# Second layer of the expert by seven products of halves, its weights' sums formed in the third chunk

## The chip, the cores and the metric

The kernel runs on one core of a Trainium2 chip. A core has a tensor engine for matmuls (PE, its weight loads shown apart as PEld), a vector engine (DVE), a scalar engine (ACT), GpSimd (POOL) and SyncE (SP), which issues nearly all DMAs here. The engines share a memory on the chip (SBUF) and the accumulators of the matmuls (PSUM, used here as banks of 128 x 512 floats). Each engine works through its own instructions in the order in which they were written, and waits on semaphores for the others. The metric is the device time of one execution in microseconds (us).

## What is computed

First an attention with a window of 32 positions and 32 global tokens (8 batches, 8 heads, head size 64). Then, on its 4608 output rows of 512 numbers, an RMS norm and a gated layer in float32:

```python
rms = np.sqrt(np.mean(x * x, axis=-1, keepdims=True) + 1e-06)
xn = x / rms * rms_g
g = xn @ w_gate                      # 512 x 1536
silu = g * (1.0 / (1.0 + np.exp(-g)))
val = xn @ w_val                     # 512 x 1536
return (silu * val @ w_out).astype(np.float32)   # w_out: 1536 x 512
```

"First layer" means the products with `w_gate` and `w_val` below, "second layer" that with `w_out`.

## The kernel before

**Numbers in halves of precision.** Every operand of a large product is held as two fp16 parts, a high one and a low one (what the high one leaves out). A product is three matmuls: high by high, low by high, high by low.

**Chunks.** The rows go in nine chunks, counted from 0: chunks 0 to 7 have 512 local rows each, chunk 8 the 256 global rows. So the fourth chunk is chunk 3, and `EARLY` (2) is the third. Chunk 0 and the attention of chunks 0 and 1 stand in an order written out by hand (`ORDER`). From chunk 1 on a loop at L1455 writes a list of work items for PE per chunk: first-layer items and then second-layer items. Between two items, `slot` (L1406) issues the steps of the next chunks' attention that are due; then come the steps of the next chunk's norm (`at`), what takes the item's result out of PSUM (`rest`), and the delayed steps of the pair before (`tail`).

**First layer of chunks 2 to 7** (`moe_pair`, L1088). A pair g of two 128-wide blocks f of the 1536 columns is done by seven products of halves, in the order 6, 1, 5, 7, 2, 3, 4, one work item each of 12 matmuls with 256 columns (L1108). The products share three banks: 7 and 4 go on top of 6, 3 on top of 5, 2 on top of 1, after ACT or DVE has read the value under them (L1124 to L1154). Their weights' sums were formed in chunk 1 and stored in HBM (`fold`, `wd`); `fetch` (L1079) brings them back, four tiles a pair, into the twelve buffers `wf`, which also hold the intermediate results s, u and v. `feed` (L1450) issues the fetches at fixed items.

**Between the layers.** A pair's tail runs at the items of the next pair: `gate` (L1158, DVE), `inner` (L1162, DVE, times the constant c_h and v), `high` (L1170, ACT) and `low` (L158, POOL through the helper `sub`; L156 where it is DVE). The last pair's tail runs in the first items of the second layer.

**Second layer** (`moe_block`, L1258). For each of the four blocks of 128 rows six items of two f, six matmuls of 512 columns each (L1266), with the weights `wo` that stay in SBUF; 24 items a chunk. `store` scales the result (L1277 on ACT, L1279 on DVE) and sends 256 KB to HBM.

**Attention of later chunks.** A local unit (`local_halves`) has loads, scores S (L665), four softmax quarters (M and N on DVE, L613; E and F on ACT, L627; D on DVE and POOL, L642; T, a transpose on DVE, L647), values A and B (L708) and the copies X and Y (L720, L721). `UNIT` says from which item on a unit may start, counted from the start of the chunk before its own, so that a negative number lies at the end of the chunk two before. S comes 8 items after the loads, the quarters 3 items apart, A 2 items after the last T. Each chunk has two such units and one of the global rows (`global_unit`).

**The norm of the next chunk** stands in the second layer at fixed distances from the chunk's end (`NORMS`): sums (L942, L944 on DVE), a matmul L953 with the root on DVE behind it (L954 to L958), then scaling, sums of halves and their two parts (`norm_halves`).

## Time and profile before

| | us |
|---|---|
| median of three runs | 934.9 |
| the three runs | 934.9, 935.76, 933.84 |
| span of the profiled execution, first to last instruction | 930.2 |
| chunk 4, first layer (488.1 to 553.4) | 65.3 |
| chunk 4, second layer (553.4 to 588.3) | 34.9 |
| chunk 7, second layer (847.9 to 879.1) | 31.2 |

The profile shows one execution. Its page gives the span from the first to the last instruction, not that execution's own time; the three times are 3.6 to 5.6 us above the span. A row of a group reads: line, engine, operation, output<-inputs, shapes, count | busy us, mean ns of one | idle time of the engine before them, and whom it waited for. In a row by line, three numbers with strokes are the shortest, the median and the longest duration in ns. In a timeline a row begins with the start and the length in us. In a row of stretches stand the stretch, its length, the busy time of each engine with the number of instructions, the granted clock of PE, the DMA share and GB/s. Consecutive instructions of DVE overlap a little: one starts before the other's recorded end.

### The profile page before, as it was taken

The page shows a single profiled execution, that of the slowest core. Times are in us where ns is not written, and L with a number is a line of the kernel's source. Part 1 is how long each engine was busy: PE and PEld are TensorE (multiplying, and loading weights), DVE is VectorE, ACT ScalarE, POOL GpSimd, SP SyncE. Part 2 cuts the span into 40 slices and gives each one's busy share as a digit, 9 for nine tenths or more (in the row PEclk, how much of TensorE's full clock was granted, in tenths as well). Part 3 has the DMA queues.
Part 4 walks back from the last instruction along what each step waited for, and adds up shares of the span by engine and source line. Part 5 has one row for each costly group of instructions (what it writes and reads, how often), then busy time and mean ns, then how long its engine had stood idle before and what let it go on. Part 6 is the DMA issues. An engine that isn't in the chain of part 4 may idle for free.

```text
span 930.2 us, 26398 instructions
## 1 busy us (share of the span) xinstructions
PE 893.9 (96%) x11028; PEld 612.2 (66%) x11028; DVE 634.0 (68%) x1603; ACT 495.4 (53%) x1232; POOL 253.8 (27%) x219
## 2 busy tenths in 40 slices
PE   5489999999999999999999999999999999999998
PEld 4444455545447885688648874788568865886584
DVE  6999987887884588557775679357846774664331
ACT  6999994555443564456344655356445732543131
POOL 0000000142423262334332353236233432332020
PEclk9699999999999999999999999999999999999999
DMA  9972533686449854495609771685349632787000
GB/s 352 407 288 96 159 120 115 209 265 198 144 119 320 282 180 147 133 299 169 213 24 279 242 238 43 200 279 184 139 136 297 190 95 79 248 273 238 35 1 23
DMA packets 83495, 173.40 MB, mean 186 GB/s; under 512 B 6705, under 2 KB 25393, under 8 KB 83377
## 3 DMA queue, kind: packets, MB, share of 16 engines
q1 hardware_dynamic: 82944, 171.40, 56.1%
q8 instruction: 86, 1.41, 0.6%
q10 hardware_dynamic: 432, 0.33, 0.1%
q14 instruction: 33, 0.26, 0.1%
HBM read 150.21 MB, written 21.50 MB: 185 GB/s over the span
## 4 chain that ended last, share of the span: by engine, by line
PE 82%; DVE 8%; DMA 4%; ACT 3%; issue 1%; POOL 1%; ACTq 0%; DVEq 0%; POOLq 0%
PE pq L1108 36%; PE po L1266 23%; PE p L1205 9%; PE a L708 4%; PE po L1333 3%; PE s L665 3%; DMA k<-in_qk_dram 2%; DMA v<-in_vw_dram 1%; DMA wr<-in_w_in_dram 1%; PE ga L838 1%; PE gs L781 1%; PE gt L824 1%; DVE wf L373 1%; ACT wr L272 1%; DVE t L1302 1%
## 5 line engine op out<-in xcount | busy, mean ns | idle before, releaser
L1108 PEld LDWEIGHTS <-wt 128*128 128x128 f16 x3024 | 292.6, 98 | 40.9 <-issue 5.3
L1266 PE MATMUL po<-wo,h 128*128 128x512 f16 x1080 | 236.2, 379 | 0.0
L1108 PE MATMUL pq<-xh,wt 128*128 128x256 f16 x1152 | 204.3, 273 | 0.0
L1266 PEld LDWEIGHTS <-h 128*128 128x128 f16 x1080 | 105.2, 98 | 123.9 <-issue 1.0
L1108 PE MATMUL pq<-xl,wt 128*128 128x256 f16 x576 | 157.0, 273 | 0.0
L1108 PE MATMUL pq<-ht,wt 128*128 128x256 f16 x1296 | 155.6, 273 | 0.9 <-issue 0.9
L642 POOL TENSOR_TENSOR e<-e,sm 128x512 f32<-128x512 f32 x48 | 50.0, 1042 | 291.4 <-DVE sm L641 287.6
L158 POOL TENSOR_TENSOR h<-t,h 128x512 f16<-128x512 f32 (+1 forms) x90 | 102.4, 1145 | 95.1 <-ACT h L1248 54.2
L1205 PE MATMUL p<-xh,wf 128*128 128x512 f16 x384 | 119.4, 382 | 6.9 <-DVE t L1302 6.3
L1205 PEld LDWEIGHTS <-wf 128*128 128x128 f16 x576 | 55.9, 99 | 74.4 <-issue 12.4
L1140 POOL TENSOR_TENSOR s<-s,s 128x512 f32<-128x512 f32 x36 | 48.2, 1339 | 190.6 <-ACT s L1137 117.9
L627 ACT ACTIVATE e<-e,sm 128x128 f32<-128x128 f32 x192 | 75.2, 393 | 36.6 <-DVE sm L613 36.5
L1170 ACT CAST h<-t 128x512 f16<-128x512 f32 x72 | 44.4, 616 | 57.3 <-DVE t L1162 56.7
L1205 PE MATMUL p<-xl,wf 128*128 128x512 f16 x192 | 73.5, 383 | 0.0
L1162 DVE SCALAR_TENSOR_TENSOR t<-t,c_h,v 128x512 f32<-128x512 f32 x72 | 70.7, 989 | 0.0
L1151 ACT ACTIVATE t<-u,half_inv 128x512 f32<-128x512 f32 x72 | 48.1, 715 | 38.7 <-DVE u L1126 28.6
L1126 DVE TENSOR_TENSOR v<-pq,s 128x512 f32<-128x512 f32 x72 | 49.6, 689 | 24.5 <-PE pq L1108 23.8
L1139 DVE TENSOR_TENSOR s<-pq,s 128x512 f32<-128x512 f32 x36 | 24.9, 691 | 44.3 <-PE pq L1108 42.2
L1133 ACT COPY s<-pq 128x512 f32<-128x512 f32 x36 | 21.0, 584 | 51.3 <-PE pq L1108 51.3
L613 DVE CUSTOM_DVE_ANT_0 e<-s,maskb 128x128 f32<-128x128 f32 x192 | 45.8, 278 | 2.8 <-PE s L665 2.8
L1126 DVE TENSOR_TENSOR u<-pq,s 128x512 f32<-128x512 f32 x36 | 24.9, 691 | 32.9 <-PE pq L1108 24.5
L1158 DVE SCALAR_TENSOR_TENSOR t<-t,u 128x512 f32<-128x512 f32 x72 | 46.9, 679 | 0.5 <-ACT t L1151 0.5
(352 smaller groups left out, 1281.5 us busy)
## 6 DMA issues: line engine op xcount, KB each, us to landing
wt<-wd SPq DMA_DIRECT2D x120, 512.0 KB, 4.8
wr<-in_w_in_dram SPq DMA_DIRECT2D x24, 512.0 KB, 9.9
k<-in_qkb_dram SPq DMA_DIRECT2D x24, 448.0 KB, 6.6
gkq<-in_gkq_dram SPq DMA_DIRECT2D x16, 576.0 KB, 6.5
wt<-wd SPq DMA_DIRECT2D x36, 256.0 KB, 4.7
out_dram<-o SPq DMA_DIRECT2D x34, 256.0 KB, 2.1
v<-in_vb_dram SPq DMA_DIRECT2D x24, 352.0 KB, 7.1
v<-in_vw_dram SPq DMA_DIRECT2D x16, 512.0 KB, 9.7
```

Source lines behind the costliest of these rows:

```text
L158: nc.gpsimd.tensor_tensor(dst, a, b, ALU.subtract)
L613: nc.vector.tensor_tensor_reduce(out=e[:, g, :], in0=ps[:, g * P : (g + 1) * P], in1=late["mask"][:, m * P : (m + 1) * P], scale=-0.125, s ...
L627: nc.scalar.activation(e[:, g, :], e[:, g, :], AF.Exp, bias=sm[:, 0, j + g : j + g + 1], scale=-1.0, accum_out=sm[:, 1, j + g : j + g + 1],)
L642: nc.gpsimd.tensor_tensor(e, e, r.unsqueeze(2).to_broadcast([P, 4, P]), ALU.mult)
L1108: nc.tensor.matmul(ps[:, j * HT : (j + 1) * HT], w[:, j, i, k * P : (k + 1) * P], x[:, k * HT : (k + 1) * HT], start=first, stop=(p in end ...
L1126: nc.vector.tensor_tensor(o, ps, x.rearrange("p (j n) -> p j n", j=2), ALU.add)
L1140: nc.gpsimd.tensor_tensor(s(6), s(6), s(1), ALU.add)
L1151: nc.scalar.activation(t, st["u"][:, j, :], AF.Tanh, scale=half_inv[:, f : f + 1])
L1158: nc.vector.scalar_tensor_tensor(t, t, 1.0, u, ALU.add, ALU.mult)
L1162: nc.vector.scalar_tensor_tensor(t, t, c_h[:, f : f + 1], st["v"][:, j, :], ALU.mult, ALU.mult)
L1205: nc.tensor.matmul(ps[:, :n], rows[:, a, o : o + P], ch[z][k][:, :n], start=(k == 0 and i == 0), stop=(k == NK - 1 and i == 2),)
L1266: nc.tensor.matmul(ps[0], ch["h", f][:, a, j * P : (j + 1) * P], wo[f][:, z, :], start=(f == 0 and q == 0), stop=(f == NF - 1 and q == 2),)
```

## The change

From chunk 3 on, the second layer is done by seven products of halves too (`moe_out`): a block (p, g) of the list `BLOCKS` is six matmuls with 256 columns (three in chunk 8), and a work item has two blocks, so 21 items a chunk instead of 24. Products 1, 5 and 6 run side by side over g; then 2 goes on top of 1's bank, 7 on 6, 3 on 5, 4 on 6. ACT takes out 1, 6 and 2, DVE adds the others (`rest`). The stationary operand is a half of the inner values or one of four sums of halves (`out_parts`): DVE forms the sums, ACT takes the high parts, POOL the low ones (DVE for the last pair). The moving operand is a tile of the weights: a half of `wo` or a sum of halves. These sums are formed in chunk 2 (`fold_out`: POOL, DVE, ACT, POOL) and stored in HBM with the plain halves (`wa`, `wb`); `fetch_out` brings them back in eleven fetches a chunk. All fetches now have a due item, nine items ahead (`LEAD`), 19 in chunk 8. The results are stored in two transfers of 512 KB. Two powers of two in the scaling are changed, and attention's starts move from -26, 2, 12 to -29, -1, 9.

```diff
-    UNIT = {2: (0, 20), 3: (-26, 2, 12)}
+    UNIT = {2: (0, 20), 3: (-29, -1, 9)}
     FOLD = 6
+    LEAD = 9
...
-        nc.vector.tensor_scalar(x2, g2[:, 1:2], ginv, 2.0**-16, ALU.mult, ALU.mult)
+        nc.vector.tensor_scalar(x2, g2[:, 1:2], ginv, 2.0**-14, ALU.mult, ALU.mult)
...
-        power(gp[0], 1, 15, k_o)
+        power(gp[0], 1, 13, k_o)
...
+    wa = dram.tile([P, NF // 2, 3, 2, HT], F16, tag="wa", bufs=1, name="wa")
+    wb = dram.tile([P, 4, NF // 2, 2, HT], F16, tag="wb", bufs=1, name="wb")
+    ALONG, AFTER = (1, 5, 6), (2, 7, 3, 4)
+    BLOCKS = [(p, g) for g in range(NF // 2) for p in ALONG]
+    BLOCKS += [(p, g) for p in AFTER for g in range(NF // 2)]
+
+    def fold_out(g):
+
+        st = {}
+
+        def total():
+            w = wo[2 * g][:, 0], wo[2 * g + 1][:, 0]
+            t = st["t"] = pool.tile([P, 1024], F32, tag="wo", bufs=7, name=f"os{g}")
+            for j in range(2):
+                nc.gpsimd.tensor_tensor(
+                    t[:, j * DM : (j + 1) * DM], wo[2 * g + j][:, 0], wo[2 * g + j][:, 1], ALU.add
+                )
+
+        def sums():
+            a = st["t"].rearrange("p (q n) -> p q n", q=4)
+            for q, r in ((0, 1), (1, 3), (3, 0), (2, 3)):
+                x, y = (a[:, r], a[:, q]) if q < 2 else (a[:, q], a[:, r])
+                nc.vector.tensor_tensor(a[:, q], x, y, ALU.subtract)
+
+        def high():
+            d = pool.tile([P, 4, 2, HT], F16, tag="wf", bufs=NF, name=f"od{g}")
+            st["d"] = d
+            nc.scalar.copy(d[:, :, 0, :], st["t"].rearrange("p (q n) -> p q n", q=4))
+
+        def low():
+            d = st["d"]
+            sub("P", d[:, :, 1, :], st["t"].rearrange("p (q n) -> p q n", q=4), d[:, :, 0, :])
+
+        def store():
+            d = st["d"]
+            nc.sync.dma_start(wa[:, g, 1:3], d[:, 0::3])
+            nc.sync.dma_start(wb[:, 1::2, g], d[:, 1:3])
+            nc.sync.dma_start(wa[:, g, 0], wo[2 * g][:, :, :HT])
+            for z in range(2):
+                w = wo[2 * g + 1][:, :, z * HT : (z + 1) * HT]
+                nc.sync.dma_start(wb[:, 2 * z, g], w)
+
+        return {0: total, 2: sums, 4: high, 5: low, 8: store}
...
-    def moe_pair(ch, g):
+    def fetch_out(c, k):
+        t = pool.tile([P, 4, 2, HT], F16, tag="wf", bufs=NF, name=f"wu{c}_{k}")
+        if k < 5:
+            n = min(4, 18 - 4 * k)
+            src = wa.rearrange("p g q a n -> p (g q) a n")[:, 4 * k : 4 * k + n]
+        else:
+            n = 4
+            src = wb.rearrange("p q g a n -> p (q g) a n")[:, 4 * k - 20 : 4 * k - 16]
+        nc.sync.dma_start(t[:, :n], src)
+        for i in range(n):
+            chunks[c]["wu", (4 * k if k < 5 else 4 * k - 2) + i] = t[:, i]
+
+    def moe_pair(ch, g, parts):
...
+        def formed(j):
+            f, v = 2 * g + j, st["v"][:, j, :]
+            nc.vector.scalar_tensor_tensor(
+                v, st["t", j], c_h[:, f : f + 1], v, ALU.mult, ALU.mult
+            )
+
+        sums, units, splits = out_parts(ch, g, lambda: (st["v"], st["u"]), SL)
...
-        if g == NF // 2 - 1:
+        if parts:
+            ch["tail", g] = [
+                lambda: (gate(0), gate(1)),
+                lambda: (formed(0), formed(1)),
+                lambda: (sums(0), units(0)),
+                lambda: (sums(1), units("P")),
+                lambda: splits(0),
+                lambda: splits("P"),
+            ]
+            if g == NF // 2 - 1:
+                ch["tail", g] = [
+                    lambda: (gate(0), gate(1)),
+                    lambda: (formed(0), formed(1)),
+                    lambda: (sums(0), sums(1), units(0)),
+                    lambda: (splits(0), units("P")),
+                    lambda: splits("V"),
+                    lambda: None,
+                ]
+        elif g == NF // 2 - 1:
...
+    def out_parts(ch, g, tiles, n):
+
+        w, st = n // 2, {}
+
+        def of(t):
+            return t.rearrange("p j (z n) -> p j z n", z=2)
+
+        def sums(i):
+            v, s = (of(t) for t in tiles())
+            if i == 0:
+                nc.vector.tensor_tensor(s[:, 0, 0], v[:, 0, 1], v[:, 1, 1], ALU.add)
+                nc.vector.tensor_tensor(s[:, 1, 0], v[:, 0, 0], v[:, 0, 1], ALU.subtract)
+            else:
+                nc.vector.tensor_tensor(s[:, 0, 1], s[:, 0, 0], v[:, 0, 0], ALU.subtract)
+                nc.vector.tensor_tensor(s[:, 1, 1], v[:, 1, 0], s[:, 0, 1], ALU.subtract)
...
+        def units(on):
+            v = tiles()[0]
+            if not on:
+                hi, lo = st["u"] = both("hu", "wo", 7)
+                for j in range(2):
+                    ch.setdefault("hp", {})[1 + j, g] = [x[:, j, :w] for x in (hi, lo)]
+                ch["hp"][4, g] = [x[:, 1, w:] for x in (hi, lo)]
+                nc.scalar.copy(hi, v)
+            else:
+                hi, lo = st["u"]
+                sub(on, lo[:, :, :w], v[:, :, :w], hi[:, :, :w])
+                sub(on, lo[:, 1, w:], v[:, 1, w:], hi[:, 1, w:])
+
+        def splits(on):
+            s = tiles()[1]
+            if not on:
+                hi, lo = st["s"] = both("hs", "h", NF // 2)
+                for p, j, z in ((5, 0, 0), (6, 0, 1), (7, 1, 0), (3, 1, 1)):
+                    ch["hp"][p, g] = [x[:, j, z * w : (z + 1) * w] for x in (hi, lo)]
+                nc.scalar.copy(hi, s)
+            else:
+                hi, lo = st["s"]
+                sub(on, lo, s, hi)
+
+        return sums, units, splits
+
+    def moe_out(ch, c, n, row):
+
+        st, w, nj = {}, n // 2, n // 256
+        onto = {2: 1, 7: 6, 3: 5, 4: 6}
+
...
+        def products(i):
+            for b in (2 * i, 2 * i + 1):
+                p, g = BLOCKS[b]
+                ps, first = bank(p)
+                hi, lo = ch["hp"][p, g]
+                u = ch["wu", b]
+                for j in range(nj):
+                    for a, x in ((0, hi), (0, lo), (1, hi)):
+                        nc.tensor.matmul(
+                            ps[:, j * HT : (j + 1) * HT],
+                            x[:, j * P : (j + 1) * P],
+                            u[:, a, :],
+                            start=first,
+                            stop=(p in (2, 3, 4) and g == NF // 2 - 1 and a == 1),
+                            skip_group_check=True,
+                        )
+                        first = False
...
+        def put(z, h, p, x):
+            o = result(z, h)
+            ps = part(p).rearrange("p (j n) -> p j n", j=nj)
+            if x is None:
+                nc.scalar.mul(o, ps, inv_k)
+            else:
+                nc.vector.scalar_tensor_tensor(
+                    o, ps, inv_k, x.rearrange("p (j n) -> p j n", j=nj), ALU.mult, ALU.add
+                )
+
+        def store(z):
+            to = out[row + z * w : row + (z + 1) * w, :].rearrange("(j p) d -> p j d", p=P)
+            nc.sync.dma_start(to, st["o", z][:, :nj, :])
+
+        def rest(p):
+            if p == 1:
+                st["s"], st["q"] = tile("os"), tile("oq")
+                nc.scalar.mul(flat("s", 0), part(1), inv_k)
+            elif p == 6:
+                nc.scalar.mul(flat("q", 0), part(6), inv_k)
+                nc.vector.scalar_tensor_tensor(
+                    flat("s", 1), part(5), inv_k, flat("s", 0), ALU.mult, ALU.add
+                )
+                nc.gpsimd.tensor_tensor(flat("q", 0), flat("q", 0), flat("s", 0), ALU.add)
+            elif p == 2:
+                put(0, 0, 2, None)
+            elif p == 7:
+                put(1, 1, 7, flat("s", 1))
+            elif p == 3:
+                put(0, 1, 3, flat("q", 0))
+                store(0)
+            elif p == 4:
+                put(1, 0, 4, flat("s", 0))
+                store(1)
...
+            if f % 2:
+                sums, units, splits = out_parts(ch, f // 2, lambda: (v, u), n)
+                later(1, lambda: (sums(0), sums(1), units(0)))
+                later(2, lambda: splits(0))
+                later(3, lambda: (units("P"), splits("V")))
...
-            (lambda: half(1, 1), inner),
+            (lambda: half(1, 1), formed if c == B else inner),
...
+    outs = [fold_out(g) for g in range(NF // 2)]
+
+    per = {c: 63 if c > EARLY else 66 for c in range(EARLY, B)}
+    per[1] = 72
+    start = {c: sum(per[x] for x in range(1, c)) for c in range(1, NCH)}
+    ring = []
+    for c in range(EARLY, NCH):
+        for g in range(NF // 2):
+            for i in range(2 if c == B else 4):
+                due = start[c] + (8 * g + 2 * i - 19 if c == B else 7 * g + 2 * i - LEAD)
+                ring.append((due, lambda c=c, g=g, i=i: fetch(c, g, i)))
+        if c > EARLY:
+            for k in range(11):
+                due = start[c] + (48 if c == B else 42) + 2 * k - (19 if c == B else LEAD)
+                ring.append((due, lambda c=c, k=k: fetch_out(c, k)))
 
     def feed():
-        if ring:
-            fetch(*ring.pop(0))
+        n = 0
+        while ring and ring[0][0] <= tick[0] and n < 2:
+            ring.pop(0)[1]()
+            n += 1
...
+            work = [w for g in range(NF // 2) for w in moe_pair(ch, g, c > EARLY)]
         else:
-            work = [w for f in range(NF) for w in moe_f(ch, f, n, "P")]
+            work = [w for f in range(NF) for w in moe_f(ch, c, f, n, "P")]
         first = len(work)
-        work += [w for j in range(n // P) for w in moe_block(ch, j, row)]
+        if c > EARLY:
+            work += moe_out(ch, c, n, row)
+        else:
+            work += [w for j in range(n // P) for w in moe_block(ch, j, row)]
         total = len(work)
+        assert c == B or total == per[c]
...
-            if EARLY <= c < B and k >= 7 and k % 7 < 5 and k <= first + 4:
+            if EARLY <= c < B and k >= 7 and k % 7 < 6 and k <= first + 5:
                 ch["tail", k // 7 - 1][k % 7]()
...
-                if -12 <= k - total < -4:
-                    feed()
-            elif c < B and k < first and k % 7 in (1, 3, 5, 6):
-                feed()
-            elif c == B - 1 and first <= k < first + 8:
-                feed()
+            if c == EARLY:
+                for g, steps in enumerate(outs):
+                    if k - 9 * g in steps:
+                        steps[k - 9 * g]()
+            feed()
```

53 lines of the change are left out of this document (48 added, 5 removed).

## Prediction

> **What bounds the kernel now.** I read the page first, then its chain, then the stretches between the PE's changes of line.
>
> ```profile
> span 930.2 us, 26398 instructions
> ...
> PE 893.9 (96%) x11028; PEld 612.2 (66%) x11028; DVE 634.0 (68%) x1603; ACT 495.4 (53%) x1232; POOL 253.8 (27%) x219
> ...
> PE 82%; DVE 8%; DMA 4%; ACT 3%; issue 1%; POOL 1%; ACTq 0%; DVEq 0%; POOLq 0%
> PE pq L1108 36%; PE po L1266 23%; PE p L1205 9%; PE a L708 4%; PE po L1333 3%; PE s L665 3%; DMA k<-in_qk_dram 2%; DMA v<-in_vw_dram 1%; DMA wr<-in_w_in_dram 1%; PE ga L838 1%; PE gs L781 1%; PE gt L824 1%; DVE wf L373 1%; ACT wr L272 1%; DVE t L1302 1%
> ```
>
> The reader sees a PE that works 96% of the span, and a chain that is mostly PE. The second layer (L1266) is 23% of it. The next view is the busy time by stretch: chunk 4's first layer, its second layer, the second layers of chunks 6 and 1.
>
> ```profile
> core 0: us, PE busy (x) PEld busy (x) DVE busy (x) ACT busy (x) POOL busy (x), PEclk, DMA share, GB/s
> 488.10:553.40 65.30, 65.30 (x1031) 57.15 (x1028) 39.53 (x96) 35.74 (x90) 26.05 (x22) 1.00 0.79 243
> 553.40:588.30 34.90, 34.90 (x356) 17.23 (x354) 27.53 (x76) 15.68 (x51) 11.47 (x9) 1.00 0.23 87
> 753.60:784.80 31.20, 31.20 (x148) 14.33 (x146) 20.62 (x35) 8.44 (x15) 7.02 (x5) 1.00 0.15 51
> 250.40:286.30 35.90, 35.49 (x358) 17.45 (x354) 29.17 (x77) 16.12 (x51) 12.40 (x10) 1.00 0.59 189
> ```
>
> The PE never stops in chunk 4. But in the second layer DVE is busy 27.53 of 34.90 us: the engine that must supply the new operands is the fullest after PE, exactly where the change shortens PE.
>
> **The saving on PE.** The timeline of PE in that second layer, and of the same place in chunk 1:
>
> ```profile
> 553.45 7.93 PE L1266 MATMUL po<-wo,h 128*128 128x512 f16 x36
> 562.75 2.06 PE L665 MATMUL s<-k,q 64*32 64x128 f32 x128
> 586.85 1.54 PE L708 MATMUL a<-et,v 32*64 32x256 f32 x80
> 588.32 1.48 PE L1108 MATMUL pq<-ht,wt 128*128 128x256 f16 x12
> 284.88 1.52 PE L708 MATMUL a<-et,v 32*64 32x256 f32 x78 [0.41 <-DVE et L647]
> ```
>
> One 512-column matmul ends 0.379 us after its start (next fence), so 36 of them start every (7.93 - 0.38)/35 = 0.2157 us; 256 columns, 0.273 us each, start every (1.48 - 0.27)/11 = 0.1097 us. Halving the columns costs almost nothing per column. A chunk's 144 matmuls of 512 (31.06 us; the row of chunk 6 shows 31.20) become 42 blocks of 6 with 256 columns: 252 x 0.1097 = 27.64. Saved: 3.42 us in each of chunks 3 to 7, and 72 x 0.2157 - 126 x 0.1097 = 1.71 in the last. Sum **-18.8 us**.
>
> **What the halves cost.** Durations by line, shortest, median and longest, or the group's mean:
>
> ```profile
> L1266 PE MATMUL po<-wo,h 128*128 128x512 f16 x1080 | 236.2, 379 | 0.0
> L1108 PE MATMUL pq<-ht,wt 128*128 128x256 f16 x1296 | 155.6, 273 | 0.9 <-issue 0.9
> L1158 DVE SCALAR_TENSOR_TENSOR t<-t,u x72: 648/684/693, 298.1 to 849.3; 128x512 f32<-128x512 f32 x72
> L1162 DVE SCALAR_TENSOR_TENSOR t<-t,c_h,v x72: 737/746/1756, 299.3 to 850.6; 128x512 f32<-128x512 f32 x72
> L1126 DVE TENSOR_TENSOR v<-pq,s x72: 678/692/693, 293.6 to 848.1; 128x512 f32<-128x512 f32 x72
> L1057 DVE TENSOR_TENSOR ws<-wq x12: 412/418/421, 152.4 to 254.6; 128x256 f32<-128x256 f32 x12
> L156 DVE TENSOR_TENSOR wq<-ws,wq x12: 1218/1264/1991, 154.3 to 257.4; 128x1024 f16<-128x1024 f32 x12
> L158 POOL TENSOR_TENSOR h<-t,h x90: 670/1159/2141, 181.3 to 911.7; 128x512 f16<-128x512 f32 x78, 128x256 f16<-128x256 f32 x12
> L1140 POOL TENSOR_TENSOR s<-s,s x36: 1266/1272/1757, 289.8 to 840.8; 128x512 f32<-128x512 f32 x36
> L642 POOL TENSOR_TENSOR e<-e,sm x48: 1032/1041/1048, 180.3 to 741.2; 128x512 f32<-128x512 f32 x48
> ```
>
> Per pair of f-blocks the new tail keeps two gates (L1158) and two products like L1162, adds four sums of 256 columns (like L1057), turns POOL's two subtractions of 512 (2 x 1.16) into units of 512 and 256 (1.16 + 0.67) and splits of 1024 (estimate 2.1, two of 256 to 512 steps of 0.49 on top of 1.16). ACT's two casts become two of 1024; ACT has half of its time free. What makes this dear is that POOL and DVE exclude each other:
>
> ```profile
> 544.90 1.27 POOL L1140 TENSOR_TENSOR s<-s,s 128x512 f32<-128x512 f32 x1 [2.79 <-issue]
> 546.13 1.16 POOL L158 TENSOR_TENSOR h<-t,h 128x512 f16<-128x512 f32 x1
> 546.17 1.67 DVE L1162 SCALAR_TENSOR_TENSOR t<-t,c_h,v 128x512 f32<-128x512 f32 x1
> 569.14 1.04 POOL L642 TENSOR_TENSOR e<-e,sm 128x512 f32<-128x512 f32 x1 [9.71 <-DVE sm L641]
> 569.38 1.35 DVE L1000 TENSOR_TENSOR x<-x 128x512 f32<-128x512 f32 x1
> 534.65 0.65 DVE L1158 SCALAR_TENSOR_TENSOR t<-t,u 128x512 f32<-128x512 f32 x1
> 535.22 0.74 DVE L1162 SCALAR_TENSOR_TENSOR t<-t,c_h,v 128x512 f32<-128x512 f32 x1
> 535.88 0.17 DVE L641 RECIPROCAL sm<-sm 128x4 f32<-128x4 f32 x1
> ```
>
> POOL's subtraction ends at 547.29; the DVE product that began 0.04 us after it ends at 547.84, some 0.55 later, and L1000 does so after L642. DVE operations with both inputs in SBUF wait for a running POOL operation; those with one input in PSUM (L1126, at most 693 ns) never do. Dense DVE operations start 0.57 and 0.66 us apart, about 0.085 less than they last.
>
> So I count what holds that shared resource per pair, against the 7 x 12 x 0.1097 = 9.2 us that PE needs. Before: gates 1.2, products 1.3, POOL 1.27 + 2.32 = 6.1. After: 1.2 + 1.3 + 4 x 0.34 + 1.27 + 1.83 + 2.1 = 9.1; and in the two pairs over which a softmax runs (four L642 of 1.04 in a chunk), 11.2. That is 2 us too much in each, **4 us per first layer of chunks 3 to 6**, since a bank is written again only two products after DVE or ACT reads it (L1139, L1126 on banks 5 and 6): PE tolerates about 2 us of lag. Bounds 0 (lag is made up between) and 6. Four chunks: **+16**.
>
> The Trainium skill's page "SBUF — State Buffer", section "Who interferes with whom", gives the rule: a DVE instruction with two SBUF inputs and a GpSimd instruction that reads SBUF take one port pair as an exclusive lock, whoever starts first. The rows of L1162 agree (746 alone, up to 1756). No gate of the trace ever met POOL (at most 693); by the rule gates block too, and without it the crowded pair holds 10.0 instead of 11.2 and this term would be 6 instead of 16.
>
> **The second layer of chunks 3 to 5.** The diff also moves attention: with 63 items and starts of -29 and 9, the next scores L665 are issued in the first item after the first layer (before: the seventh), and attention's values L708, which wait for the last transpose L647, after the 18th of 21 items (before: the 24th). PE would be there after 18 x 1.316 + 2.06 + 0.14 (the norm's matmul) = 25.9 us. DVE before:
>
> ```profile
> 583.21 0.71 DVE L647 STREAM_TRANSPOSE et<-e 128x512 f32<-128x512 f32 x1 [1.15 <-POOL e L642]
> 586.96 0.75 DVE L1279 TENSOR_SCALAR o<-po,kk 128x512 f32<-128x512 f32 x1 [3.04 <-PE po L1266]
> ```
>
> That transpose ended 30.5 us after the layer's start, with 27.53 - 0.75 = 26.8 us of DVE work ahead of it. After: less the copy of L721 (0.42), a result (0.66) and the last low part (0.68), plus the last sums 1.36, splits 1.26 and two recombinations from PSUM 1.32, is 29.0. PE waits at least 29.0 - 25.9 = 3.1 us; with the same 3.7 us of DVE gaps (round trips to PE, POOL and ACT) 6.8. I take 5: **+15** for three chunks. Part of it falls earlier: the last splits stand behind gates, norm sums and norm scaling, and block 17 of 42 needs them. In chunk 6, without softmax, only that counts: queue 0.2 + 0.6 + 1.3 + 1.2 + 1.3 + 3.15 + 1.4 + 1.3 + 1.3 = 11.8 against PE's 8 x 1.316 + 0.14 = 10.7, plus at most two port waits of 1.0: **+2** (1 to 3). The norm's share comes from these rows (558.13 to 559.47, 561.55 to 564.70):
>
> ```profile
> 558.13 0.70 DVE L942 STREAM_TRANSPOSE st<-sq 128x512 f32<-128x512 f32 x1
> 559.47 0.68 DVE L156 TENSOR_TENSOR h<-t,h 128x512 f16<-128x512 f32 x1
> 561.55 0.17 DVE L954 TENSOR_SCALAR nt<-ss 128x16 f32<-128x16 f32 x1 [1.40 <-PE ss L953]
> 564.70 0.25 DVE L613 CUSTOM_DVE_ANT_0 e<-s,maskb 128x128 f32<-128x128 f32 x1
> ```
>
> **Chunks 1 and 2.** They keep the old second layer, but the values come three items (3.9 us) earlier, and in chunk 1 they already waited 0.41 us for the transpose; DVE is idle 6.7 us there, so 0 to 4, taken **+2**. Chunk 2 also forms the weights' sums: per 9 items two POOL additions and a subtraction of 1024 (2 x 1.2 + 2.1; nearest rows L1140, L158) and four DVE sums, 5.9 us on the shared port, 4.6 per pair. 8.2 + 4.6 = 12.8 against 9.2 in two pairs: 7.2; and in its second layer 30.5 + 1.4 against 21 x 1.295 + 2.2 = 29.4: 2.5. Together **+10** (0 to 13).
>
> **What costs nothing.** DMA: 42 blocks of 128 KB are 5.5 MB more per chunk, in 11 fetches nine items (11.8 us) ahead where a 512 KB fetch lands in 4.8:
>
> ```profile
> wt<-wd SPq DMA_DIRECT2D x120, 512.0 KB, 4.8
> ```
>
> They fall mostly into stretches with a DMA share of 0.23; 11 fetches of 0.52 MB in 31 us add 184 GB/s, some 0.6 by the 0.79 that carried 243, so SP's queue stays under full. The fetches now pass attention loads and the stores (two of 512 KB for four of 256 KB) on SP, and a fetch that waits for a buffer holds up those behind it; buffers come free at least an item before. If that cover went, each late fetch would cost PE a few us. Changed powers of two cost nothing.
>
> **Sum.** -18.8 + 16 + 15 + 2 + 2 + 10 = +26. It holds against the profiled execution, whose span is 930.2; the page does not say its own time, and the three times lie 3.6 to 5.6 above that span. From the median 934.9: **961 us**.
>
> **Rivals.**
> *DVE's lag is absorbed* (port waits fall where nobody waits): the pair term and chunk 2's fall to 1, the second layers to their lower bounds 3 x 3.1 + 1 with 0 in chunk 1: -18.8 + 11.3 = -7.5, **927**. For it: DVE is busy only 39.53 of 65.30 us in the first layer. Against it: the rows of waits above.
> *The full saving*: DVE stays ahead everywhere, 934.9 - 18.8 = **916**. Against it: 29.0 us of queued work ahead of a wait at 25.9.
> *The upper bounds meet*: -18.8 + 24 + 20 + 3 + 4 + 13 = +45, **980**.
> *A draw*: stalls of about 19 us.
>
> **Chances.** Forecast (945 to 985) 0.60, between it and the draw 0.07; draw (within 0.2%, about what a measurement tells from no change) 0.04; lag absorbed 0.21; full saving 0.08. So faster 0.29, same 0.04, slower 0.67. The range 919 to 982 leaves out the full saving and little above the upper bounds. With both signs open, the likeliest case alone reaches from 945 to 982.
>
> **What would show it.** PE waiting for DVE splits at the 17th block and for L647 before L708 in chunks 3 to 5; waits on DVE results in the first layers of chunks 3 to 6 (none now); gates and sums longer than 0.7 and 0.42 while POOL runs; chunk 7 and the last one shorter by 3.4 and 1.7. I am wrong if DVE, though full, stays within two items of PE, or if the new operands are late from HBM.

## The result, and the profile after

The changed kernel takes **996.6 us** (median; 996.2 to 1000.0) where the kernel before takes 935.2 (933.8 to 935.8): a ratio of 1.067, 95% interval 1.065 to 1.069. The forecast was 961, its range 919 to 982. The sign was right, and the size was not: the forecast had +26 us, the runs show +61.

In the changed kernel the lines have moved: the first layer's matmuls are L1165, the new second layer's L1354, attention's values L709, its transposes L648; the gates are L1215, the products with `c_h` L1234, the four sums L1291 to L1295, ACT's casts L1309 and L1321, the subtractions for low parts L159 on POOL and L157 on DVE, the recombination of the results on DVE L1385.

The page of the changed kernel, first its totals:

```profile
span 994.1 us, 28060 instructions
...
PE 903.2 (91%) x11622; PEld 678.0 (68%) x11622; DVE 784.5 (79%) x1790; ACT 526.6 (53%) x1245; POOL 346.2 (35%) x273
```

DVE is busy 150 us longer than before with 187 instructions more, which is 0.8 us each. Some of the added ones are longer by nature, but the sums (L1291 to L1295) take 0.52 to 0.76 us in the mean, where one takes 0.41 when nothing holds it. The busy times of the whole stretch from chunk 1's second layer to chunk 8's, of the kernel before and after:

```profile
250.40:910.60 660.20, 658.63 (x8240) 483.87 (x8237) 416.74 (x1012) 312.04 (x808) 227.26 (x194) 1.00 0.56 181
```

```profile
252.10:976.50 724.40, 666.45 (x8784) 541.88 (x8776) 563.61 (x1191) 342.10 (x818) 318.52 (x246) 0.98 0.67 216
```

PE stood still 660.20 - 658.63 = 1.6 us before and 58.0 after: 56.4 of the 64.2 us that this stretch grew by are waits. And PE's busy time, which should have fallen by 5 x 3.42 = 17.1, rose by 7.8. The granted clock (0.98 instead of 1.00) says why in part.

The same view by stretch, of after: chunk 2's first layer; chunk 4's first and second layer; the second layers of chunks 6 and 7.

```profile
292.70:363.10 70.40, 64.60 (x932) 56.02 (x931) 58.78 (x114) 37.55 (x91) 46.77 (x33) 1.00 0.77 243
...
520.60:592.20 71.60, 66.12 (x933) 56.18 (x932) 57.44 (x116) 36.66 (x86) 34.37 (x26) 1.00 0.76 249
592.20:632.60 40.40, 36.20 (x561) 30.06 (x560) 32.89 (x83) 19.26 (x55) 15.23 (x12) 0.92 0.51 163
...
817.90:851.70 33.80, 29.52 (x256) 25.42 (x254) 26.06 (x42) 11.04 (x17) 11.00 (x8) 0.95 0.51 167
...
917.30:945.10 27.80, 27.80 (x257) 24.77 (x255) 16.37 (x35) 9.18 (x16) 9.94 (x9) 1.00 0.64 220
```

Chunk 4's first layer took 65.30 us of unbroken PE before and takes 71.60, its DVE 57.44 instead of 39.53. Of these stretches only chunk 7's second layer, with no attention and no next first layer of 512 rows beside it, is what the matmuls alone make it: 27.80 where 27.64 was forecast.

What PE waited for, in the view of waits (us in total, times, longest), behind the 17.3 us for the very first loads:

```profile
...
PE pq L1165 <- DVE s L1196: 10.7, 10, 3.3
PE pr L1354 <- DVE hs L157: 7.7, 4, 2.2
PE pr L1354 <- ACT hs L1321: 7.1, 3, 3.2
PE pq L1165 <- DVE v L1183: 7.0, 10, 1.4
...
PE a L709 <- DVE et L648: 6.1, 3, 2.2
PE a L709 <- issue: 4.5, 3, 1.7
PE pq L1165 <- ACT s L1190: 3.8, 5, 0.9
```

The reader sees the first layer waiting for a bank that DVE or ACT has not read out yet (L1196, L1183, L1190), the second layer waiting for a split (L157, L1321), attention's values waiting for a transpose, or for nothing the profile names. All but the last were named in the forecast, but not all lie where it put them: the three waits for the transpose end at 245.3, 284.1 and 400.0 us, in chunks 1 and 2, and chunks 3 to 5, for which the forecast had them, show none.

How a gate gets late, in the timeline of POOL and of DVE, chunk 4's first layer:

```profile
543.19 2.14 POOL L159 TENSOR_TENSOR hs<-u,hs 128x1024 f16<-128x1024 f32 x1 [1.44 <-ACT hs L1321]
545.38 1.63 POOL L1197 TENSOR_TENSOR s<-s,s 128x512 f32<-128x512 f32 x1
...
543.77 3.79 DVE L1215 SCALAR_TENSOR_TENSOR t<-t,u 128x512 f32<-128x512 f32 x2 [0.54 <-ACT t L1208]
547.48 1.40 DVE L1234 SCALAR_TENSOR_TENSOR v<-t,c_h,v 128x512 f32<-128x512 f32 x2
```

Two gates that take 1.3 us when free take 3.79, and end 0.55 us after POOL's second operation ended at 547.01. Everything behind them on DVE, the reading out of banks above all, is late by 2.5 us.

### The profile page after: what moved, and what is told of

It reads as the page before. It is cut to its first block, busy times and chain, and to the rows that moved or that the text cites. A ratio compares the mean times of both kernels' runs of the same rounds, so it can differ in the third digit from the quotient of the medians.

```text
span 994.1 us, 28060 instructions
## 1 busy us (share of the span) xinstructions
PE 903.2 (91%) x11622; PEld 678.0 (68%) x11622; DVE 784.5 (79%) x1790; ACT 526.6 (53%) x1245; POOL 346.2 (35%) x273
## 3 DMA queue, kind: packets, MB, share of 16 engines
q1 hardware_dynamic: 100448, 209.94, 64.2%
## 5 line engine op out<-in xcount | busy, mean ns | idle before, releaser
L1165 PEld LDWEIGHTS <-wt 128*128 128x128 f16 x3024 | 294.2, 98 | 68.9 <-issue 30.6
L1165 PE MATMUL pq<-xh,wt 128*128 128x256 f16 x1152 | 206.4, 273 | 11.5 <-DVE s L1196 10.7
L1165 PE MATMUL pq<-ht,wt 128*128 128x256 f16 x1296 | 156.5, 274 | 11.0 <-DVE v L1183 7.0
L1165 PE MATMUL pq<-xl,wt 128*128 128x256 f16 x576 | 157.3, 273 | 0.0
L1354 PE MATMUL pr<-wu,hs 128*128 128x256 f16 x792 | 98.3, 279 | 15.3 <-DVE hs L157 7.7
L1354 PEld LDWEIGHTS <-hs 128*128 128x128 f16 x792 | 78.4, 100 | 28.6 <-DVE hs L157 8.4
L628 ACT ACTIVATE e<-e,sm 128x128 f32<-128x128 f32 x192 | 75.1, 393 | 40.6 <-DVE sm L614 40.5
L1215 DVE SCALAR_TENSOR_TENSOR t<-t,u 128x512 f32<-128x512 f32 x72 | 81.2, 1163 | 11.3 <-ACT t L1208 11.1
L159 POOL TENSOR_TENSOR hu<-v,hu 128x512 f16<-128x512 f32 (+1 forms) x60 | 61.4, 1043 | 48.4 <-ACT hu L1309 48.4
L1354 PE MATMUL pr<-wu,hu 128*128 128x256 f16 x594 | 76.5, 279 | 1.3 <-ACT os L1396 0.6
L1507 PE MATMUL po<-wo,h 128*128 128x512 f16 x288 | 64.7, 380 | 3.8 <-DVE o L1520 1.3
L1354 PEld LDWEIGHTS <-hu 128*128 128x128 f16 x594 | 59.3, 101 | 11.2 <-issue 2.5
L159 POOL TENSOR_TENSOR hs<-u,hs 128x1024 f16<-128x1024 f32 x25 | 53.4, 2135 | 35.7 <-ACT hs L1321 35.3
L1309 ACT CAST hu<-v 128x1024 f16<-128x1024 f32 x30 | 31.3, 1043 | 52.9 <-DVE v L1234 52.9
L1183 DVE TENSOR_TENSOR v<-pq,s 128x512 f32<-128x512 f32 x72 | 49.1, 682 | 9.9 <-PE pq L1165 9.9
L1321 ACT CAST hs<-u 128x1024 f16<-128x1024 f32 x30 | 31.4, 1048 | 46.6 <-DVE u L1295 46.6
```

The source lines that it names most:

```text
L159: nc.gpsimd.tensor_tensor(dst, a, b, ALU.subtract)
L628: nc.scalar.activation(e[:, g, :], e[:, g, :], AF.Exp, bias=sm[:, 0, j + g : j + g + 1], scale=-1.0, accum_out=sm[:, 1, j + g : j + g + 1],)
L1165: nc.tensor.matmul(ps[:, j * HT : (j + 1) * HT], w[:, j, i, k * P : (k + 1) * P], x[:, k * HT : (k + 1) * HT], start=first, stop=(p in end ...
L1183: nc.vector.tensor_tensor(o, ps, x.rearrange("p (j n) -> p j n", j=2), ALU.add)
L1215: nc.vector.scalar_tensor_tensor(t, t, 1.0, u, ALU.add, ALU.mult)
L1309: nc.scalar.copy(hi, v)
```

## The experiments

My theory after the result: the added load of DVE and POOL in the first layers (four sums, longer low parts, and the port they share) makes PE wait, and the moved starts of attention add to it. Rivals: the transfers (SP's new order of fetches), and the new second layer itself. The medians of before beside these runs are 934.1 to 936.1, single runs of it 931.2 to 937.8. e1 to e4 and e6 to e8 ran once each, so a few us between two of them say nothing.

**The added low parts, and the added sums, each left out.** e1: POOL forms no low parts in chunks 3 to 7 (the products use the high part twice); what stays is DVE's low parts of the last pair's splits. e2: the four sums of DVE are left out there.

e1:

```diff
+                if n == SL:
+                    lo = hi
-            else:
+            elif n < SL:
                 hi, lo = st["u"]
...
+                if n == SL and g < NF // 2 - 1:
+                    lo = hi
...
-            else:
+            elif on == "V":
                 hi, lo = st["s"]
```

e2:

```diff
             v, s = (of(t) for t in tiles())
+            if n == SL:
+                return
```

> Leaves out the low parts that POOL forms for the second layer's operands in chunks 3 to 7 (the units of every pair and the splits of all but the last pair of a chunk); the matmuls run as often as before, with the high part in their place. DVE's and ACT's work is unchanged. Theory A (POOL and DVE exclude each other at the operations with two SBUF inputs): gates and sums come back to their free lengths (gates from a mean of 1163 to under 850 ns), chunks 3 to 6 lose 4 to 6 us each, 970 to 980 us in all, chunk 2 unchanged at 116. Rival B (DVE has simply too many instructions, POOL does not matter): gates stay where they are and the time stays within 4 us of 996.6. Rival C (the moved attention alone): the same as B.

> Leaves out the four sums of halves that DVE forms per pair in chunks 3 to 7; the splits are taken from the unsummed tile, POOL, ACT and PE do as much as before. Theory A: the sums hold the shared port 1.4 us a pair and wait for POOL on top, chunks 3 to 6 lose 6 to 9 us each, 960 to 972 us in all. Rival B (number of DVE instructions): the bare 1.4 us a pair, of which only the two crowded pairs and the last one count, some 4 us a chunk, 980. Rival C (the moved attention alone): within 8 us of 996.6.

Measured: **973.7** and **969.2**, both in the theory's ranges; the mean gate of e1 is 812 ns. A third run leaves out both (e11):

> The changed kernel without the POOL low parts and without the four DVE sums in the first layers of chunks 3 to 7 (e1 and e2 together; the second layers then multiply stale or high halves, the products are as many). Theory: the loss of the 512-row chunks is the added load of DVE and POOL in the first layers, so that e1's 22.9 us and e2's 27.4 us nearly add: 943 to 953, first layers of chunks 3 to 6 at 64 to 66.5 us, half clock mostly in chunks 1 and 2. Rival: the second layers' own work on DVE and ACT (splits of U) and the order of the transfers carry a part that neither e1 nor e2 took: 956 to 966, second layers of chunks 3 to 5 still above 36 us.

Measured: **958.9**, in the rival's range. The stretches of chunk 4's first layer in e1, e2 and e11 (columns as above: length, then PE, PEld, DVE, ACT, POOL):

```profile
515.70:584.60 68.90, 65.55 (x934) 56.14 (x933) 50.59 (x117) 37.17 (x87) 15.18 (x12) 1.00 0.77 257
```

```profile
513.70:580.50 66.80, 64.68 (x933) 56.08 (x931) 46.34 (x97) 38.79 (x90) 33.22 (x27) 1.00 0.79 265
```

```profile
511.70:577.70 66.00, 64.57 (x934) 56.12 (x932) 41.25 (x97) 38.87 (x90) 16.11 (x13) 1.00 0.80 274
```

This is the clearest reading of the study. e2 and e11 have the same 97 DVE instructions; with POOL's low parts beside them they take 46.34 instead of 41.25 us, so 5.1 us of DVE's busy time are nothing but waiting for POOL. The sums alone add 9.3 (50.59), both together 16.2 (57.44). In the length of the layer: +0.8 for the low parts, +2.9 for the sums, **+5.6** for both (in the four layers of chunks 3 to 6 together +3.4, +9.0 and +22.6). Together they cost more than their sum: in time, 958.9 grows by 10.3 for the low parts and by 14.9 for the sums, and by 37.7 for both.

**Attention and norm three items later** (e3), and that with e1's edit (e6):

```diff
-    UNIT = {2: (0, 20), 3: (-29, -1, 9)}
+    UNIT = {2: (0, 20), 3: (-26, 2, 12)}
...
-        gaps = NORM.get(c, NORMS)
+        gaps = NORM.get(c, NORMS if c <= EARLY else (19, 18, 16, 14))
```

> Undoes one part: attention starts at -26, 2, 12 again, and in chunks 3 to 6 the next norm's steps stand three items nearer to the chunk's end, so that both lie as far behind the first layer's end as before the change. Theory (the last pair's sums and splits stand behind norm and softmax in DVE's queue): the wait for the last splits (2.2 us and more a chunk) and its half-clock stretch go, chunks 3 to 6 lose 3 to 6 us each and chunks 1 and 2 some 3 each, 968 to 982 us; the waits of the first layers for DVE stay. Rival (only the load of the shared port counts, wherever the steps stand): the waits move, the time stays above 990.

> Both edits of the first two of these kernels that touched chunks 3 to 6: POOL's low parts of the second layer's operands left out (high part in their place) and attention and norm as far behind the first layer as before. Theory: two causes that add up, chunks 3 to 6 come to 99 to 102 us each (before 100.2, after 112), 950 to 960 us in all; what is left sits in chunk 2. Rival (each edit removes the same waits): no better than 968.

Measured: **982.1**, the upper edge of what the theory allowed, and **970.3**, which is the rival's: with e1's edit in place, the later start gives 3 us, no more than single runs differ by. The waits move instead of going, and half clock, which the theory had going with them, rises from 27.3 us in the changed kernel to 37.6 in e3 (more on it below). In e3 those for splits are no longer among the large ones, but the second layer now waits for the recombination of its results on DVE:

```profile
PE pr L1354 <- DVE oo L1385: 14.1, 3, 5.2
```

and chunk 2's first layer takes 76.9 us instead of 70.4, which eats up the 4.5 us that chunk 1's second layer gives (36.1 instead of 40.6); about 1.3 us of both are attention's matmuls that stand on the other side again.

**The forming of the weights' sums** (e4: the tiles go to HBM unsummed):

```diff
...
-        return {0: total, 2: sums, 4: high, 5: low, 8: store}
+        return {8: store}
```

> Leaves out the forming of the second layer's weight sums in chunk 2 (POOL, DVE and ACT); plain halves are stored in their place, every transfer and matmul stays. Theory: chunk 2 falls from 116.3 to 103 to 106 us (its first layer to about 65, the waits for the weights' sums and POOL in its second layer go), 983 to 987 us in all. Rival (chunk 2 is late because attention's values were moved forward): chunk 2 stays above 111, 992 or more in all.

Measured: **985.4**, and 105.7 us for chunk 2, both as the theory had it. So the forming costs 11.2 us, 3.7 of them in chunk 2's first layer and 6.9 in its second. From the other end, e11 without the forming too (e12):

> As e11, and the forming of the weights' sums in chunk 2 left out too (e4's edit: the weights' tiles go to HBM unsummed). What is left of the change is the seven products, their splits and their transfers. Theory: e4's 11.2 us come on top, 932 to 942, and the distance to the full saving of 18.8 us (916) is what the second layers' splits, chunk 1's shift and the transfers cost. Rival: all the loss was the added first-layer and forming work, and the time is 916 to 924.

Measured: **947.5** (two runs, 944.8 and 950.2), 11.4 less than e11, but neither prediction holds: with all the added work of POOL and DVE in first layers gone, the seven products, with the moved starts and the transfers that came with them, still lose 12 us to before where they should gain 19.

**What is left in e12.** Three more runs took e12 and changed the attention's starts (e13, the diff of e3), the fetches' lead (e14), or both (e15); e16 is the whole change with the longer lead.

```diff
-    LEAD = 9
+    LEAD = 12
```

> As e12 (products alone: no POOL low parts, no sums in the first layers, weights' tiles unsummed), with e3's starts: attention and norm three items later in chunks 3 to 6. If the attention's early start makes the 31 us: the waits of L709 for L648 and for nothing named (4.9 and 4.9 us) go from chunks 3 to 6, and the time is 932 to 941. If it is SP's order or the second layer's own hand-overs: 944 to 950.

> As e12, with the fetches issued up to 12 items ahead in place of 9, starts as in the change. If SP's order (late transfers of attention's tiles or of the weights) makes the 31 us: 932 to 941. If it is the early start: 944 to 950.

> As e12, with the later starts and the 12 items ahead together. If one of the two alone makes the loss: as the better of e13 and e14, within 3 us. If both have a part: 922 to 932. If the second layer's own hand-overs (banks that wait for ACT's copies, L1396 and L1398 in the change) make it: 940 to 950.

> The whole changed kernel, with the fetches issued up to 12 items ahead in place of 9. If late transfers have a part in its loss: 978 to 990. If the lag of DVE and POOL alone makes it: 993 to 1000.

Measured, in this order: **948.4**, **955.6**, **943.7** and **1009.2**. Neither the starts nor the lead alone is the cause: e13 stays where e12 was, e14 and e16 are slower than without the longer lead, by 8 and 13 us, and beyond both of their ranges. With the later starts the longer lead helps by 5, little more than the runs of one kernel differ by, which puts e15 into its third range; but that range was given for banks that wait for ACT's copies, and in e15 the largest named wait but the start-up's is again a result's recombination on DVE:

```profile
PE pr L1361 <- DVE oo L1392: 11.5, 3, 3.8
...
PE a L709 <- issue: 4.2, 3, 2.3
PE s L666 <- issue: 4.1, 3, 1.6
```

In e12 it was ACT's copies (L1403 and L1405: 5.8 us in six waits), which are not among e15's waits. What the early starts cost is plain where the layer itself did not change: the second layers of chunks 1 and 2, still 24 items, take 41.3 and 39.6 us in e12 and 35.9 and 34.9 in e13 (36.0 and 34.9 before); of the 10 us, 2.6 are moved matmuls, and in e13 other stretches took the rest back, with 30.7 us of half clock where e12 has 3.4. So the rest of some 30 us is a set of waits of 1 to 4 us that change places with every shift; which of them must go first stayed open.

**The port by itself.** e7 takes the kernel before and lets POOL do its last subtraction of each pair but the last of a first layer four times: 3.5 us more of POOL reading SBUF, with the same values. e8 puts eight fills there instead, 4.6 us of POOL that only write.

e7:

```diff
-            lambda: low(1),
+            lambda: (low(1), low(1), low(1), low(1)),
```

e8:

```diff
-            lambda: low(1),
+            lambda: ([nc.gpsimd.memset(st["h"][:, 1, 1, :], 0.0) for _ in range(8)], low(1)),
```

> The kernel before, with POOL's last subtraction of each pair but the last of a chunk done four times: 3.5 us more POOL work a pair that reads and writes SBUF, not one instruction more on DVE, ACT or PE. Theory A (POOL alone can do it, by the shared port): gates meet POOL, DVE's operations with two SBUF inputs lengthen, PE waits for DVE in chunks 2 to 6, 3 to 5 us a chunk, 945 to 958 us. Rival B (it takes DVE's additional instructions): within 2 us of 934.1.

> The kernel before, with eight fills by POOL of the tile that its last subtraction of each pair then writes: more POOL work that only writes SBUF and reads nothing. If it is reading that holds the port, DVE's operations that meet a fill keep their free length (746 for the product with c_h and v) and the time stays within 3 us of 934.1. If any POOL operation does, they lengthen as in the kernel with four subtractions.

Measured: **961.8** (the theory's sign, some 4 us beyond its range) and **975.1**, far from the theory's "within 3". The timeline of e8 shows both halves of the answer:

```profile
526.25 4.59 POOL L1180 MEMSET h<- 128x512 f16 x8
530.92 1.16 POOL L158 TENSOR_TENSOR h<-t,h 128x512 f16<-128x512 f32 x1
...
529.72 1.28 DVE L1158 SCALAR_TENSOR_TENSOR t<-t,u 128x512 f32<-128x512 f32 x2
530.92 1.71 DVE L1162 SCALAR_TENSOR_TENSOR t<-t,c_h,v 128x512 f32<-128x512 f32 x1
```

Two gates run beside the fills in 1.28 us, untouched; the product that meets the subtraction takes 1.71 instead of 0.74. So it is POOL's reading that holds DVE back. But the fills cost 40 us almost without holding DVE (busy 40.03 us in chunk 4's first layer, 39.53 before), since POOL's own queue got late: the softmax's L642 and through it the transposes, which waited 6.2 us for it in the kernel before, and DVE's operations behind them.

```profile
DVE et L647 <- POOL e L642: 53.0, 16, 5.8
...
PE a L708 <- DVE et L647: 16.3, 7, 2.8
PE pq L1108 <- DVE s L1139: 9.4, 5, 1.9
```

What follows: occupancy of POOL costs time here in two ways, and e7, which does both, can't say how much of its 27 us is the port. Its transposes wait 40.5 us for L642, and DVE's busy time in chunk 4's first layer is 41.01 us, only 1.5 more than before, where the layer is 5.7 longer; so the larger part looks like POOL's lateness, which is argued and not shown. The port's part is shown in DVE's busy time (the 5.1 us above), not in the kernel's.

**The chunks where the cover holds.** Seven products in chunks 7 and 8 alone, the weights' sums formed over chunks 2 to 6, attention's starts as in the kernel before (e5):

```diff
-    UNIT = {2: (0, 20), 3: (-29, -1, 9)}
+    UNIT = {2: (0, 20), 3: (-26, 2, 12)}
+    LATE = 6
+    PLAN = ((2, 12), (3, 12), (4, 12), (5, 12), (6, 12), (6, 54))
...
-            work = [w for g in range(NF // 2) for w in moe_pair(ch, g, c > EARLY)]
+            work = [w for g in range(NF // 2) for w in moe_pair(ch, g, c > LATE)]
...
-            if c == EARLY:
-                for g, steps in enumerate(outs):
-                    if k - 9 * g in steps:
-                        steps[k - 9 * g]()
+            for (pc, pk), steps in zip(PLAN, outs):
+                if c == pc and k - pk in steps:
+                    steps[k - pk]()
```

> Seven products in the second layer of chunks 7 and 8 alone, where no local softmax runs beside them; the six formings of weight sums are spread, one at item 12 of each of chunks 2 to 6 and one at item 54 of chunk 6; attention's starts are those of before. Theory (the saving on PE is real wherever DVE and POOL have room): chunks 1 to 6 as before, the second layer of chunk 7 31.2 to 27.8 us, of chunk 8 15.7 to 14.1, and up to 2.5 us given back in chunk 7's first layer: 930 to 933 against 934.1 to 935.2. Rival (any forming of halves costs more than the 3.4 us): 935 or more.

Measured: **938.5**, ratio 1.0042 (1.0027 to 1.0057), in the rival's range. The second layers gave their 2.8 and 1.6 us, and first layers took them back: chunk 2's 70.0 instead of 65.6, chunk 7's 69.6 instead of 63.1, with PE waiting for the global loads:

```profile
PE gs L784 <- DMA gkq<-in_gkq_dram: 3.5, 2, 2.0
...
PE pq L1167 <- issue: 2.1, 1, 2.1
PE a L711 <- issue: 1.9, 1, 1.9
```

The new due times had reordered SP's queue. The global loads at the start of chunk 7, in the kernel before and in e5 (the chunk starts at 784.8 and 784.6):

```profile
786.18 0.92 SPq L759 DMA_DIRECT2D gkq<-in_gkq_dram  x2
```

```profile
794.99 1.52 SPq L762 DMA_DIRECT2D gkq<-in_gkq_dram  x2
```

e9 puts the fetches back to the places of before, and e10 takes chunk 7 out of it:

e9:

```diff
...
+    pos = [start[2] - 11 + j for j in range(8)]
+    pos += [start[c] + k + 1 for c in range(2, B) for k in range(42) if k % 7 in (1, 3, 5, 6)]
+    ring = [(d, lambda x=x: fetch(*x)) for d, x in zip(pos, wts)]
...
```

e10:

```diff
-    LATE = 6
+    LATE = 7
```

> Seven products in the second layers of chunks 7 and 8 alone, as in e5, but SP issues the weight tiles of the first layers at the places of before: eight in the last items of chunk 1, then four in every seven items of a first layer; the tiles of sums of chunk 7 take the eight places that are left. The sums of weights are formed in chunks 2 to 6 as in e5. Theory: e5's second layers were 2.8 and 1.6 us shorter, and the order of the issues on SP took it back (global loads 8.8 us later, TensorE waiting 1.65 and 2.37 us for them in chunk 7, half clock behind the waits). Then chunk 2's first layer is back at 65.5 to 66.5 us, chunk 7's at 63 to 65, half clock at 0 to 3.5 us, and the time is 930 to 933 where before has 934.6. Rival: the added low parts and sums of chunk 7, and the forming of weights' sums in chunks 2 to 6, cost what the products give, whatever SP's order: 934.5 to 938.5, with chunk 7's first layer still above 67 us.

> As e9, with seven products in the second layer of chunk 8 alone, so that no first layer has the added low parts and sums of a 512-row chunk. Theory of e9: chunk 8's second layer gives 1.6 us as in e5, chunk 7 is as before (63.1 and 31.2 us), and the time is 932.5 to 934 where before has 934.6. Rival: the forming of weights' sums in chunks 2 to 6 costs more than 1.6 us by itself: 935 to 938. The distance to e9 is what chunk 7 gives or takes: by the theory e9 is 0.5 to 2.8 faster, by the rival of e9 it is the slower of the two.

Measured: **930.6**, ratio 0.9959 (0.9945 to 0.9972), and **931.9**, ratio 0.9976 (0.9964 to 0.9988): e9 in its theory's range, e10 0.6 us below it. Chunk 2's first layer, chunk 7's first layer and chunk 7's second layer in e9:

```profile
288.40:354.60 66.20, 65.35 (x1031) 57.26 (x1028) 41.55 (x100) 36.94 (x91) 30.75 (x25) 1.00 0.83 263
787.40:851.40 64.00, 63.55 (x751) 54.76 (x750) 49.50 (x83) 31.62 (x55) 27.30 (x20) 1.00 0.73 235
851.40:880.10 28.70, 28.42 (x257) 24.78 (x256) 17.26 (x36) 9.16 (x16) 9.45 (x9) 1.00 0.62 205
```

With the order of before, the two first layers lose 0.6 and 0.9 us instead of 4.4 and 6.5: e5 and e9 differ in nothing but the items at which SP issues the fetches, and so in their order among its other transfers, and in 7.9 us. In chunk 7, beside which no local attention runs, the sums and low parts fit beside PE although DVE has 49.50 us of work in 64.00. e9 is faster than both kernels. Between e9 and e10 lie 1.3 us with intervals that overlap, so what chunk 7 adds is likely, not shown.

## Why the prediction was wrong

Stretch by stretch, us, PE's own saving taken out (a loss is positive). Some 98 of attention's small matmuls (1.31 us for 96 of them) moved from a first layer into the second layer ahead of it, so the split between the two kinds is off by 1.3 us a chunk, their sum is not: like for like, the first layers of chunks 3 to 6 lost about 32 us, the second layers of chunks 3 to 5 about 21.5.

| term | forecast | measured |
|---|---|---|
| PE's saving, chunks 3 to 8 | -18.8 | -18.8 taken; -3.4 and -1.6 seen in chunks 7 and 8 |
| first layers of chunks 3 to 6 | +16 | 4.9 + 6.3 + 9.5 + 6.2 = +26.9 |
| second layers of chunks 3 to 5 | +15 | 8.8 + 8.9 + 7.7 = +25.4 |
| second layer of chunk 6 | +2 | +6.0 |
| up to chunk 1's end | +2 | 1.7 + 4.6 = +6.3 |
| chunk 2 | +10 | 4.8 + 11.0 = +15.8 |
| chunk 7's first layer | 0 | +2.5 |

The span grew by 63.9; the terms sum to 64.1. Of the 1.7 ahead of chunk 1's second layer none need be the change: e7 and e8, whose program is that of the kernel before up to there, took 1.1 and 2.4 (what 1.4 of it is stands in the last section).

**Right:** the saving on PE (27.80 for 27.64); that DVE, not PE, sets the pace of chunks 3 to 5; the places of two of the three kinds of waits (splits in the second layer, banks in the first layers); chunk 6's second layer waiting for splits without any softmax; the cost of forming the sums in size (11.2 and 11.4), though partly by luck: the forecast had 7.2 in chunk 2's first layer and 2.5 for all else in its second, where 4.8 and 11.0 were measured, and e4 puts 3.7 and 6.9 of these down to the forming. Right too is the disputed rule, that gates wait for POOL as well. The gates take 81.2 us in after, 1163 ns in the mean, and 55.9 us in e1:

```profile
L1215 DVE SCALAR_TENSOR_TENSOR t<-t,u 128x512 f32<-128x512 f32 x72 | 81.2, 1163 | 11.3 <-ACT t L1208 11.1
```

```profile
L1215 DVE SCALAR_TENSOR_TENSOR t<-t,u 128x512 f32<-128x512 f32 x72 | 55.9, 812 | 8.0 <-ACT t L1208 7.9
```

The Trainium skill's page "SBUF — State Buffer", section "Who interferes with whom", says so, and adds that a GpSimd instruction that only writes does not block. The fills of e8 agree with this second half: twelve gates ran beside fills for 0.57 us or more and took 681 to 689 ns.

The trace of before could have settled the rule ahead of the forecast, which said that no gate of it ever met POOL. It looked at DVE's side alone. Six gates did, and there POOL was the one that waited:

```profile
554.59 1.28 DVE L1158 SCALAR_TENSOR_TENSOR t<-t,u 128x512 f32<-128x512 f32 x2
555.54 1.46 POOL L725 TENSOR_TENSOR sq<-sq,sq 128x512 f32<-128x512 f32 x1 [2.19 <-ACT sq L723]
```

The second gate of the first row starts at 555.19. Five of the six operations are this L725, begun 0.35 us into the gate: it takes 1457 to 1459 ns there, where its median is 1273. All six POOL operations end 1.12 us after the gate does.

**Wrong, the first-layer term** ("4 us per first layer of chunks 3 to 6"). I added up what holds the shared port, compared it with PE's 9.2 us per pair, and charged only the excess. That treats DVE as a store of work that catches up. e1 refutes it: with POOL busy 15.18 us, less than the 26.05 before, and thus far less on the port, the sums alone made the layer 2.9 us longer. DVE executes in order, and a bank has to be read within two products; 9.3 us more of queue are late at such a point long before any resource is full. And e1 and e2 beside the whole change show that the two loads together cost more than their sum.

**Wrong, the second layers** ("I take 5"). The term is a wait for L647 before L708, 3.1 to 6.8 us in each of chunks 3 to 5, and this wait is not there. The three that the view of waits has lie in chunks 1 and 2, and the first of them is in the kernel before too (2.06 us at 245.0). In chunks 3 to 5 PE was late itself, held earlier by the splits, which I had counted as part of the same wait. In chunk 2 and in chunk 4 of the changed kernel:

```profile
399.96 2.44 PE L709 MATMUL a<-et,v 32*64 32x256 f32 x78 [2.22 <-DVE et L648]
```

```profile
607.16 0.28 PE L1354 MATMUL pr<-wu,hs 128*128 128x256 f16 x1 [1.94 <-ACT hs L1321]
609.63 2.52 PE L1354 MATMUL pr<-wu,hs 128*128 128x256 f16 x11 [2.19 <-DVE hs L157]
...
625.13 2.23 PE L709 MATMUL a<-et,v 32*64 32x256 f32 x80
```

PE reaches the values of chunk 4 32.9 us after the layer's start (592.25), where the forecast had it there at 25.9. The two waits for splits are 4.1 of these 7 us, and the half clock behind them some 2.4 (an estimate: half of the 4.9 us that PE worked in it). DVE's side was forecast well: the last transpose ends after 33.5 us, forecast 29.0 to 32.7, and since PE came just as late, its 80 matmuls take 2.23 us instead of 1.54 and no more. Over chunks 3 to 6 PE waited 7.7 us for DVE's splits and 7.1 for ACT's, which had waited for DVE's last sums.

A second part of the loss was in no term. In e11 the waits for splits are down to 0.2 us a layer, and the second layers of chunks 3 and 4 still take 36.1 us where 34.9 - 3.4 = 31.5 would be free: 1.3 are the moved matmuls, 2.0 the waits for ACT's copies out of banks 1 and 6.

**Wrong, what "costs nothing".** I held that SP's queue stays under full and that the fetches are hidden. The share of DMA was no problem (0.76 in chunk 4's first layer, 0.79 before); the order was: between e5 and e9 it alone is 7.9 us. Its part in the whole change was not isolated; the longer lead made that kernel slower.

**Not seen at all: the clock.** Longer stalls of PE are often followed by 3.41 us at half clock (when, is worked out in the last section). Around the wait for splits in chunk 4's second layer, four windows of that length:

```profile
600.85:604.27 3.42, 3.42 (x34) 3.07 (x32) 3.15 (x9) 0.83 (x5) 1.70 (x2) 1.00 0.76 216
604.27:607.68 3.41, 1.23 (x10) 0.70 (x8) 3.38 (x11) 1.62 (x4) 1.04 (x1) 1.00 0.63 213
607.68:611.09 3.41, 1.46 (x7) 1.01 (x8) 3.41 (x9) 1.44 (x8) 0.00 (x0) 0.50 0.28 90
611.09:614.51 3.42, 3.42 (x18) 2.29 (x16) 3.39 (x10) 1.82 (x6) 1.82 (x2) 0.50 0.39 132
```

In the last, PE never stops and does 18 matmuls where the first has 34. From chunk 1 on, the changed kernel has 27.3 us of half clock, the kernel before none; PE was busy 23.8 of them, so about 11.9 us of its work were lost. This is a price on stalls of about two microseconds that the forecast's waits did not carry.

Put together, the 61 us are: all that is left in e12 (products, their hand-overs, moved starts, transfers) +12 (the products' saving is -19, so a loss of 31, open in its parts), forming +11, the sums +15, the low parts +10, and +13 that only sums and low parts together make. Each step is a difference of the runs e12, e11, e1, e2 and after; e12's two runs lie 5.5 us apart, so its step and the next are known to a few us only.

## What to carry to other kernels

An engine that works in order can hold up others long before it is full (DVE was busy 50.59 of 68.90 us in e1): count for each queue not its total against the bottleneck's, but the time by which the next operand or bank is due, with the others' work in front of it, and price a stall of PE at its length plus what the slower clock takes behind it. Take a saving first where the helpers have nothing else to do (here the last two chunks: -4 us, with attention's starts and the fetches' places left as they were, while the whole change cost +61). Look for waits between DVE and POOL on both sides: in these traces the one that began later waits. When a change adds transfers, keep the places of the old ones on their queue; a share of bandwidth that looks free says nothing about the order.

## What the hardware showed that I had not expected

The granted clock is decided in windows of 3.41 us that follow each other without regard to the program: in each trace all changes of the clock from 60 us on lie on one grid of that step, to within 2 ns. Over the traces of all eighteen kernels, from 120 us on, with the windows laid by each trace's own changes of clock, every window in which PE stood still for 2.0 us or more in all (59 of 59) was followed by one at half clock; between 1.75 and 2.0 us it was 25 of 34, between 1.0 and 1.75 us 13 of 142, and under 1.0 us 5 of some 4150. The idle time need not be in one piece: in the changed kernel a window from 396.06 with 1.07 and 1.73 us of two gaps in it was followed by half clock. And a long gap can go free when the grid cuts it: its longest stall from chunk 1 on, 3.29 us up to 336.55, falls into two windows as 1.36 and 1.94 us, and neither was followed by half clock. The same wait of 2.06 us for the transpose at 245 us was cut into 1.08 and 0.99 in the profiled run of before, which kept its clock, and lay whole in one window in e7, which lost it; chunk 1's first layer took 79.7 us in the one and 81.1 in the other, with the same program up to there. The Trainium skill's page "TensorE: Matmul & The Clock Gate", section "What's actually happening", gives the window as 3413 ns and free-running, which agrees; its section "HAM oscillation — how this bites in real kernels" puts the rule as no idle gaps above some 3.4 us, where these runs show that 2.0 us within a window suffice.
